# The second transform of a spectral and MLP mixer: radix 4 ahead of its products, or radix 2 ahead of them and radix 2 behind

## Chip, cores and metric

The kernel runs on one core of one Trainium2 chip. The time is in device microseconds for one execution. TensorE multiplies matrices, VectorE and ScalarE work element by element, SyncE (SP) issues the loads and stores. "Before" is the kernel as it stands, "after" the one with the change.

## What is computed

The input x has 2048 rows (the sequence) of 512 columns, all bf16. Two branches are mixed by a gate:

```python
g = sigmoid((x * gate_w).sum(-1, keepdims=True))
X = rfft2(x.astype(float32)) * (w_r + 1j * w_i)
a = irfft2(X, s=(2048, 512)).astype(bfloat16)
h = layernorm(x)
u = gelu(einsum("bsd,sf->bdf", h, w1) + b1)          # F = 1792
b = (einsum("bdf,fs->bds", u, w2) + b2).transpose(0, 2, 1)
out = g * a + (1 - g) * b
```

The rfft2 is a transform over the 2048 rows and one over the 512 columns. Both are done as products with tables of cosines and sines, with butterflies (additions and subtractions) around them that make the products shorter.

## The kernel before

Everything is bf16 in SBUF and fp32 in PSUM. x lies as four groups q by four remainders r by 512 columns, 128 rows in the partitions. A list of tasks is built in Python, each with an engine, an estimated duration, a priority and what it reads and writes (`Plan`, `add`). `order()` runs through these estimates and fixes the order in which each engine's instructions are written; the engines then run in that order and wait for each other through semaphores. So an edit of one task, or of its estimate, can move others.

The stages, with the names that matter here:

- **Statistics and h** (L478 to L513): mean and variance by VectorE, h mostly by ScalarE.
- **First transform** (over the rows): VectorE forms sums over q (L519 to L526, into a part of `gl`); TensorE multiplies for each r and each quarter dq of the columns (`fa`, L538 to L541), a quarter being 128 neighbouring columns; ScalarE evicts into X (L544).
- **Radix 4 over the quarters** (d4a, d4b: L551, L552, L557, L558): four additions or subtractions of 1024, 1024, 512 and 512 elements per partition for each r, in X itself and in `st`.
- **Radix 4 over r** (`radix4`, L577 to L590, once for each half lt of the frequencies, lt 1 first; L602 to L628 put the corner values right). Its results e = 0 to 3 stand in X in this order.
- **Second transform** (over the columns), `fb`: for each lt, e and c (real or imaginary part) four products, L646, L647 and twice L649, with 128, 128, 256 and 256 columns of the table `tb`; the two L649 accumulate. They write blocks of 64 columns into one bank of PSUM. ScalarE evicts each group into B and interleaves the four blocks (L653). The sixteen groups use the banks `fa` and `fb` in turn.
- **Spectral products**, all on VectorE for each lt: corner values to c0 (L770, L771), butterfly (L799, L800), preparation of W (L756 to L760, once), the multiplication by W (L807), combination (L812, L813), butterfly back (L819 to L821), then the inverse radix 4 over r (`radix4` again, L577 to L593, on B).
- **Inverse transforms**: products over the rows (L868 to L875), evictions (L881, L883), additions (L891 to L904), products over the columns (L942 to L946), evictions with the gate (L955), output additions ("es", L966 to L970).
- **MLP**: the products with w1 (L684: 14 tiles ft of the hidden width, 16 products of 512 columns each) and GELU (L700) run through the first half of the time. The products with w2 (L983: 14 for each of 16 row tiles) run through the second. Both are what the order puts between the transforms' products. `wa` and `wb` hold first w1 and then w2: SP loads w2's blocks i = 7 to 13 into `wb` when the products with the earlier contents are through.
- **Gate**: x times gate_w on VectorE (L709), sums on ScalarE (L714). The output of the MLP is scaled by ScalarE (L989), added (L995), and for the last tiles scaled and added by VectorE straight from PSUM (L1001), then stored.

Of the kernel before, what the change touches and what calls it, by code (L numbers as in the profile page):

```python
# [34 lines left out]
def make_tables():  # L35
# [49 lines left out]
                    u[:, P] = c[:, P] if lt == 0 else -n[:, P]  # L85
    ti[0, 2816:2945] = np.append(alt, 1.0)

    tb = np.zeros((P, 3, 4, 64))
    i = np.arange(64)
    for b in (0, 2):  # L90
        th = ang(p, b + 4 * i, D)
        tb[:, 0, b // 2] = np.cos(th)
        tb[:, 1, b // 2] = -np.sin(th)
    tb[:, 1, 0, 0] = alt
    tb[:, 2, 0:2] = tb[:, 0, 0:2]
    tc = np.zeros((P, 2, 3, 2, 64))
    for n, b in enumerate((1, 3)):
        th = ang(p, b + 4 * i, D)
        sg = 1.0 if b == 1 else -1.0
        tc[:, 0, 0, n] = np.cos(th)  # L100
        tc[:, 0, 1, n] = -np.sin(th)
        tc[:, 1, 0, n] = -sg * np.sin(th)
        tc[:, 1, 1, n] = -sg * np.cos(th)
    tc[:, :, 2] = tc[:, :, 0]
    cf = np.zeros((P, 4, 2))
    m = np.arange(8).reshape(4, 2)
    for r in range(4):
# [4 lines left out]
            cf[m[2, 0], r, 1], cf[m[3, 0], r, 1] = 1.0, (1.0, -1.0)[r % 2]  # L112
        if r != 0:
            cf[m[2, 1], r, 1], cf[m[3, 1], r, 1] = (0.0, -1.0, 1.0, 1.0)[r], (0.0, -1.0, -1.0, 1.0)[r]
    tb = np.concatenate([tb[:, :, 0:2].reshape(P, 384), tc.reshape(P, 768), cf.reshape(P, 8)], 1)

    tg = np.zeros((P, 642))
    sc = 2.0 / (D * S)
# [149 lines left out]
def kernel(  # L268
# [134 lines left out]
        dma(t["b1b"][0:NFT], B_b1.rearrange("(t f) -> t f", f=P))  # L403
        dma(t["b2b"][0:4], B_b2.rearrange("(q n) -> q n", q=4))
    add("SP", 1.0, ld_bias, writes=["bias"], prio=7.1, nbytes=16384, after=[a0])
    load("tb", [P, 1160], BF16, tabs["tb"], 296960, prio=9)

    def ld_wb(k, q):
        def emit():
# [46 lines left out]
        dma(t["ti"][:], tabs["ti"])  # L456
    load("tg", [P, 642], BF16, tabs["tg"], 164352, prio=29)


    HACT = set(range(NJ)) - {0, 8, 4}  # L460
    PQ0 = -0.5
    ASTAT = {12, 8}
    for r in range(4):
# [69 lines left out]
        for dq in range(4):  # L533
            def fa(r=r, dq=dq):
                pa = t["pa", r, dq] = ps([P, 2, 2, P], F32, "fa", 2)
                ta = t["ta"][:, r, :]
                w = lambda k: t["xf", r][:, k, dq * P:(dq + 1) * P]
                T.matmul(pa[:, 1], lhsT=w(2), rhs=ta[:, 256:512], start=True, stop=False)  # L538
                T.matmul(pa[:, 1], lhsT=w(3), rhs=ta[:, 384:640], start=False, stop=True)
                T.matmul(pa[:, 0, :, 0:64], lhsT=w(0), rhs=ta[:, 0:128], start=True, stop=True)  # L540
                T.matmul(pa[:, 0, :, 64:128], lhsT=w(1), rhs=ta[:, 128:256], start=True, stop=True)  # L541
            add("PE", mm(128, 128, 256, 256), fa, reads=[("xf", r % 2), ("ta", r)], writes=[("pa", r, dq)], prio=0, alloc=["fa"],
                free=["xf"] if dq == 3 else ())
            add("ACT", act(512), lambda r=r, dq=dq: A.copy(t["X"][:, :, r, :, dq, :], t["pa", r, dq][:]),  # L544
                reads=[("pa", r, dq)], writes=[("X", r, dq)], prio=0, free=["fa"])

        def d4a(r=r):
            xv = t["X"][:, :, r]
            s = t["st"][:, 1024:2048].rearrange("p (a c n) -> p a c n", a=2, c=2)
            two = lambda lo: xv[:, :, :, lo:lo + 2, :].rearrange("p a c j l -> p a c (j l)")  # L550
            V.tensor_add(s, two(0), two(2))  # L551
            V.tensor_sub(two(2), two(0), two(2))  # L552

        def d4b(r=r):
            xv = t["X"][:, :, r]
            s = t["st"][:, 1024:2048].rearrange("p (a c n) -> p a c n", a=2, c=2)
            V.tensor_add(xv[:, :, :, 0, :], s[:, :, :, 0:P], s[:, :, :, P:2 * P])  # L557
            V.tensor_sub(xv[:, :, :, 1, :], s[:, :, :, 0:P], s[:, :, :, P:2 * P])  # L558
        add("DVE", 2 * tt(1024), d4a, reads=[], writes=[("X", r, dq) for dq in range(4)] + ["sx"], prio=3.9)
        add("DVE", 2 * tt(512), d4b, reads=["sx"], writes=[("D", r)], prio=3.9)  # L560


    def radix4(view, pq, st, pqk, stk, reads, writes, prio, inverse):
        n = 512

        def parts(buf):
            v = buf().rearrange("p (m c n) -> p m c n", m=2, c=2)
            return v[:, 0], v[:, 1]

        def dst(lo, step):  # L570
            d = view().rearrange("p k c n -> p (k c) n")
            return d[:, lo:lo + step + 1:step]

        def e1():
            v = view()
            lo, hi = (v[:, 2 * i:2 * i + 2].rearrange("p m c n -> p (m c n)") for i in range(2))
            V.tensor_add(pq(), lo, hi)  # L577
            V.tensor_sub(st(), lo, hi)  # L578

        def e2():  # L580
            p, q = parts(pq)
            V.tensor_add(dst(0, 1), p, q)
            V.tensor_sub(dst(4, 1), p, q)

        def e3():
            s, u = parts(st)
            sr, ur = s[:, ::-1], u[:, ::-1]
            if not inverse:
                V.tensor_add(dst(2, 5), s, ur)
                V.tensor_sub(dst(3, 3), sr, u)  # L590
            else:
                V.tensor_add(dst(3, 3), sr, u)
                V.tensor_sub(dst(2, 5), s, ur)  # L593
        add("DVE", 2 * tt(4 * n), e1, reads=reads, writes=[pqk, stk], prio=prio)
        add("DVE", 2 * tt(2 * n), e2, reads=[pqk] + reads, writes=[writes[0]], prio=prio)
        add("DVE", 2 * tt(2 * n), e3, reads=[stk] + reads, writes=[writes[1]], prio=prio)

# [8 lines left out]
    def sp1():  # L606
# [3 lines left out]
        V.tensor_sub(sd[:, 1], sp[:, 0:2], sp[:, 2:4])  # L610
        V.tensor_add(fx[:, 0, 0], sd[:, 0, 0, 0], sd[:, 0, 1, 0])
        V.tensor_sub(fx[:, 0, 1], sd[:, 0, 0, 0], sd[:, 0, 1, 0])
        V.tensor_copy(fx[:, 1, 0], sd[:, 1, 0, 0])
        V.tensor_scalar_mul(fx[:, 1, 1], sd[:, 1, 1, 0], -1.0)
        V.tensor_scalar_mul(sd[:, 0, 0, 1], sd[:, 1, 1, 1], c)
        V.tensor_scalar_mul(sd[:, 1, 0, 1], sd[:, 0, 1, 1], -c)
        V.tensor_add(fx[:, 2, 0], sp[:, 0, 1], sd[:, 0, 0, 1])
        V.tensor_sub(fx[:, 3, 0], sp[:, 0, 1], sd[:, 0, 0, 1])
        V.tensor_sub(fx[:, 2, 1], sd[:, 1, 0, 1], sp[:, 2, 1])
        V.tensor_add(fx[:, 3, 1], sd[:, 1, 0, 1], sp[:, 2, 1])  # L620
    add("DVE", tiny(12), sp1, reads=["sp"], writes=["fx"], prio=0)

    for lt in (1, 0):
        pr = 3.0 if lt else 3.1
        radix4(lambda lt=lt: t["X"][:, lt].rearrange("p r c j l -> p r c (j l)"),
               lambda: t["xp"][:, 0:2048], lambda: t["st"][:, 0:2048], "xs", "st",
               dk + ([] if lt else ["sp"]), [("Z", lt, 0), ("Z", lt, 1)], pr, False)
    add("DVE", 0.15, lambda: V.tensor_copy(t["X"][:, 0, :, :, :, 0], t["fx"][:]), reads=["fx"],  # L628
        writes=[("Z", 0, 0), ("Z", 0, 1)], prio=3.1)

    def tbl(kind, c):
        tb = t["tb"]
        if kind < 2:
            return tb[:, 0:384].rearrange("p (c k i) -> p c k i", c=3, k=2)[:, c:c + 2, kind, :]
        v = tb[:, 384:1152].rearrange("p (g n) -> p g n", g=2)[:, kind - 2]
        return v[:, 128 * c:128 * c + 256]

    for lt in (0, 1):
        for e in (0, 2, 1, 3):
            for c in range(2):  # L640
                tag = ("fa", "fb")[c]

                def fb(lt=lt, e=e, c=c, tag=tag):
                    pb = t["pb", lt, e, c] = ps([P, 2, 4, 64], F32, tag, 2)
                    w = lambda k: t["X"][:, lt, e, c, k, :]
                    T.matmul(pb[:, :, 0, :], lhsT=w(0), rhs=tbl(0, c), start=True, stop=True)  # L646
                    T.matmul(pb[:, :, 2, :], lhsT=w(1), rhs=tbl(1, c), start=True, stop=True)  # L647
                    for k in (2, 3):
                        T.matmul(pb[:, :, 1::2, :], lhsT=w(k), rhs=tbl(k, c), start=(k == 2), stop=(k == 3))  # L649
                add("PE", mm(128, 128, 256, 256), fb, reads=[("Z", lt, e % 2), "tb"], writes=[("pb", lt, e, c)], prio=2, alloc=[tag])  # L650

                def fbev(lt=lt, e=e, c=c):
                    A.copy(t["B"][:, lt, e, 2 * c:2 * c + 2, :].rearrange("p s (i b) -> p s i b", b=4),  # L653
                           t["pb", lt, e, c][:].rearrange("p s b i -> p s i b"))
                add("ACT", act(512), fbev, reads=[("pb", lt, e, c)], writes=[("B", lt, e)], prio=1.8, free=[tag])


    def biasT():
# [105 lines left out]
    for lt in range(2):  # L764
# [8 lines left out]
        if lt == 0:  # L773
            def nyq():
# [6 lines left out]
                V.tensor_sub(nn[:, 0], na[:, 0, 1], na[:, 1, 0])  # L781
                V.tensor_add(nn[:, 1], na[:, 1, 1], na[:, 0, 0])
                V.tensor_mul(nn[:, :, 0], t["c0"][0:1, 0, 0, 1, :], wn[:, 0, 0:257:256])
            add("DVE", 3 * d1(512) + 0.1, nyq, reads=bk + [("W", 0), ("W", 1), ("c0", 0)] + pbk, writes=["nn"], prio=0.5)

        def c0b(lt=lt):
            c0, cm, ce, pm = t["c0"][:, lt], t["cm"], t["ce"][:, lt], t["wpm"]
# [46 lines left out]

    def linem():
        pl8 = t["pl8"] = ps([8, D], F32, "fa", 2)
        T.matmul(pl8[:], lhsT=t["tb"][:, 1152:1160], rhs=t["s9"][:], start=True, stop=True)
    add("PE", mm(512), linem, reads=["s9", "tb"], writes=["pl8"], prio=3, alloc=["fa"], after=[combt])
    add("ACT", act(512), lambda: A.copy(t["s8"][:], t["pl8"][:]), reads=["pl8"], writes=["s8"], prio=1.7, free=["fa"])

# [205 lines left out]
```

## Time and profile before

| | before |
|---|---|
| runs (us) | 132.31, 132.51, 132.73; median 132.51 |
| profiled execution | 132.39 us, of which the span of the trace is 130.5 |
| mean granted TensorE clock | 0.997 |
| ScalarE busy | 83.1 us |
| HBM read and written | 20.93 MB and 2.10 MB |

Times within the trace count from the start of the span. A busy time is the sum of the instructions' durations; two products overlap, so the distance from start to start ("pitch") is shorter than a duration. The rows of L646 and L649, for instance, have a mean duration of 219 and 272 ns. An idle time stands in brackets behind the instruction that ended it, with what it waited for. A line of the slices has 40 digits, each for 3.26 us, in tenths.

### The profile page before, as it was taken

The page shows a single profiled execution, that of the slowest core. Times are in us where ns is not written, and L with a number is a line of the kernel's source. Part 1 is how long each engine was busy: PE and PEld are TensorE (multiplying, and loading weights), DVE is VectorE, ACT ScalarE, POOL GpSimd, SP SyncE. Part 2 cuts the span into 40 slices and gives each one's busy share as a digit, 9 for nine tenths or more (in the row PEclk, how much of TensorE's full clock was granted, in tenths as well). Part 3 has the DMA queues.
Part 4 walks back from the last instruction along what each step waited for, and adds up shares of the span by engine and source line. Part 5 has one row for each costly group of instructions (what it writes and reads, how often), then busy time and mean ns, then how long its engine had stood idle before and what let it go on. Part 6 is the DMA issues. An engine that isn't in the chain of part 4 may idle for free.

```text
span 130.5 us, 2166 instructions
## 1 busy us (share of the span) xinstructions
PE 125.4 (96%) x780; PEld 70.7 (54%) x780; DVE 110.6 (85%) x248; ACT 83.1 (64%) x166; POOL 0.2 (0%) x4
## 2 busy tenths in 40 slices
PE   6998999999999999999999999999999999999991
PEld 2344565545544484854444555455687577655590
DVE  2689999999999997059999999999959929999961
ACT  4468989599999999996111044322499489962200
POOL 0000000000000000000000000000000000000000
PEclk9999999999999999999999999999999999999998
DMA  4999999943669536799999800000000000312331
GB/s 83 389 372 386 398 394 379 374 91 89 135 184 298 107 85 131 259 288 406 414 421 421 334 6 0 3 5 3 0 0 0 0 5 0 161 69 97 161 121 40
DMA packets 17478, 23.18 MB, mean 178 GB/s; under 512 B 1574, under 2 KB 14908, under 8 KB 17468
## 3 DMA queue, kind: packets, MB, share of 16 engines
q1 hardware_dynamic: 17180, 22.59, 50.6%
q10 hardware_dynamic: 288, 0.46, 1.3%
q8 instruction: 6, 0.10, 0.3%
q14 instruction: 4, 0.03, 0.1%
HBM read 20.93 MB, written 2.10 MB: 176 GB/s over the span
## 4 chain that ended last, share of the span: by engine, by line
PE 58%; DVE 28%; DMA 8%; issue 2%; ACT 2%; SPq 0%; DVEq 0%
PE acc L684 18%; PE acc L983 17%; DMA wa<-in_B_w_dram 5%; PE fb L684 5%; DVE xp L807 3%; DVE st L807 3%; DMA x<-in_A_x_dram 2%; PE fa L684 2%; PE fa L538 2%; DVE xp L812 2%; DVE st L578 2%; DVE B L819 2%; DVE xp L813 2%; PE fb L868 1%; PE fa L868 1%
## 5 line engine op out<-in xcount | busy, mean ns | idle before, releaser
L983 PE MATMUL acc<-gl,wb 128*128 128x512 bf16 (+1 forms) x112 | 27.4, 373 | 0.0
L983 PE MATMUL acc<-gl,wa 128*128 128x512 bf16 (+1 forms) x112 | 27.2, 372 | 0.0
L684 PE MATMUL acc<-h,wb 128*128 128x512 bf16 x112 | 25.9, 379 | 0.0
L989 ACT ACTIVATE x<-acc,ombb,omg 128x512 bf16<-128x512 f32 x14 | 10.8, 785 | 22.7 <-PE acc L983 22.7
L983 PEld LDWEIGHTS <-wb 128*128 128x128 bf16 x126 | 13.4, 114 | 10.3 <-DMA wb<-in_B_w_dram 1.2
L983 PEld LDWEIGHTS <-wa 128*128 128x128 bf16 x126 | 13.5, 114 | 9.4
L684 PE MATMUL acc<-h,wa 128*128 128x512 bf16 x64 | 17.8, 387 | 0.6 <-DVE h L505 0.6
L684 PEld LDWEIGHTS <-wb 128*128 128x128 bf16 x112 | 10.9, 98 | 11.7
L684 PEld LDWEIGHTS <-wa 128*128 128x128 bf16 x112 | 10.4, 99 | 10.8 <-issue 2.1
L700 ACT ACTIVATE gl<-acc,b1f 128x512 bf16<-128x512 f32 x11 | 7.6, 693 | 6.8 <-PE acc L684 6.8
L478 DVE BATCH_NORM_STATS2 stats<-x 128x6 f32<-128x512 bf16 x14 | 9.4, 674 | 2.2 <-DMA x<-in_A_x_dram 2.2
L544 ACT CAST X<-fa 128x512 bf16<-128x512 f32 x16 | 9.3, 582 | 2.7 <-PE fa L541 2.5
L511 ACT ACTIVATE h<-x,nmr,rstd 128x512 bf16<-128x512 bf16 x13 | 9.8, 806 | 0.4 <-DVE nmr L502 0.2
L714 ACT ACTIVATE x<-x 128x512 bf16<-128x512 bf16 x16 | 10.1, 655 | 0.0
L684 PE MATMUL fb<-h,wa 128*128 128x512 bf16 x32 | 9.4, 379 | 0.0
L955 ACT ACTIVATE B<-fb,g 128x512 bf16<-128x512 f32 x8 | 5.9, 735 | 0.0
L955 ACT ACTIVATE B<-fa,g 128x512 bf16<-128x512 f32 x8 | 5.8, 727 | 0.0
L359 PE MATMUL fa<-xp 128*128 128x512 bf16 x10 | 4.4, 632 | 1.2 <-DVE xp L320 1.2
L684 PE MATMUL fa<-h,wa 128*128 128x512 bf16 x16 | 5.6, 379 | 0.0
L653 ACT CAST B<-fb 128x512 bf16<-128x512 f32 x8 | 5.0, 628 | 0.0
L653 ACT CAST B<-fa 128x512 bf16<-128x512 f32 x8 | 4.9, 616 | 0.0
L709 DVE TENSOR_TENSOR x<-x,gw 128x2048 bf16<-128x2048 bf16 x4 | 4.8, 1216 | 0.0
(177 smaller groups left out, 230.0 us busy)
## 6 DMA issues: line engine op xcount, KB each, us to landing
wb<-in_B_w_dram SPq DMA_DIRECT2D x11, 512.0 KB
wa<-in_B_w_dram SPq DMA_DIRECT2D x7, 512.0 KB
wa<-in_B_w_dram SPq DMA_DIRECT2D x3, 896.0 KB
x<-in_A_x_dram SPq DMA_DIRECT2D x3, 512.0 KB
wb<-in_B_w_dram SPq DMA_DIRECT2D x4, 384.0 KB
out_dram<-x SPq DMA_DIRECT2D x3, 512.0 KB
rot<-dft_ti SPq DMA_DIRECT2D x1, 736.5 KB
rot<-dft_ta SPq DMA_DIRECT2D x4, 160.0 KB
```

The source lines that it names most:

```text
L478: V.bn_stats(out=t["stats"][:, j, :], in_=t["x"][:, j // 4, j % 4, :])
L511: add("ACT", 0.71, lambda j=j: A.activation(t["h"][:, j // 4, j % 4, :], t["x"][:, j // 4, j % 4, :], ActF.Identity, bias=t["nmr"][:, j:j ...
L544: add("ACT", act(512), lambda r=r, dq=dq: A.copy(t["X"][:, :, r, :, dq, :], t["pa", r, dq][:]), reads=[("pa", r, dq)], writes=[("X", r, dq ...
L653: A.copy(t["B"][:, lt, e, 2 * c:2 * c + 2, :].rearrange("p s (i b) -> p s i b", b=4), t["pb", lt, e, c][:].rearrange("p s b i -> p s i b"))
L684: T.matmul(t["u", ft][:], lhsT=w[:, j // 4, j % 4, c * P:(c + 1) * P], rhs=t["h"][:, j // 4, j % 4, :], start=(j == jorder[0]), stop=(j == ...
L700: gelus.append(add("ACT", act(512, 1) , lambda ft=ft: A.activation(t["gl"][:, ft, :], t["u", ft][:], ActF.Gelu_apprx_tanh, bias=t["b1f"][: ...
L709: add("DVE", tt(2048), lambda r=r: V.tensor_mul(t["x"][:, :, r, :], t["x"][:, :, r, :], t["gw"][:, None, :].to_broadcast([P, 4, D])), read ...
L714: A.activation(t["x"][:, q, r, :], t["x"][:, q, r, :], ActF.Copy, accum_out=t["glog"][:, 4 * q + r:4 * q + r + 1])
L807: V.tensor_mul(o, xs, w)
L955: A.activation(t["eo", j // 2][:, j % 2], t["i3", j][:], ActF.Copy, scale=t["g"][:, j:j + 1])
L983: T.matmul(t["y", j, n][:, cs], lhsT=w[:, o, 512 * q + r:512 * q + 512:4], rhs=t["gl"][:, ft, cs], start=(ft == 0), stop=(ft == NFT - 1))
L989: A.activation(tbuf(j).rearrange("p h d -> p (h d)"), t["y", j, 0][:], ActF.Identity, bias=t["ombb2"][:, j:j + 1], scale=t["omg"][:, j:j + 1])
```

## The change

In the second transform the index of the 512 columns is split as 256h + 2p + t (h and t are 0 or 1, p the partition). The first transform takes for its weights every second column (t) of one half (h) instead of 128 neighbouring columns, and is evicted into `xp` instead of X. VectorE then does a radix 2 over h alone (`d2`), from `xp` into X. The products of `fb` are four with 128 columns each, none accumulating, and each writes every second fp32 column of its 256. The evictions go back into X, and each waits for the products of both c. A radix 2 over t (`tb2`) then forms B from X: one addition of 1024 elements, two subtractions of 508 that write in reversed order, and, once per lt, six operations on the corner values. Radix 4 over r stores its results as 0, 2, 1, 3, and does lt 0 first. `tb` has 776 columns instead of 1160.

```diff
-                w = lambda k: t["xf", r][:, k, dq * P:(dq + 1) * P]
+                w = lambda k: t["xf", r][:, k, L * (dq // 2) + dq % 2:L * (dq // 2 + 1):2]
...
-            add("ACT", act(512), lambda r=r, dq=dq: A.copy(t["X"][:, :, r, :, dq, :], t["pa", r, dq][:]),
+            add("ACT", act(512), lambda r=r, dq=dq: A.copy(xe(r)[:, :, :, dq, :], t["pa", r, dq][:]),
...
-        add("DVE", 2 * tt(1024), d4a, reads=[], writes=[("X", r, dq) for dq in range(4)] + ["sx"], prio=3.9)
-        add("DVE", 2 * tt(512), d4b, reads=["sx"], writes=[("D", r)], prio=3.9)
+        def d2(r=r):
+            e, xv = xe(r), t["X"][:, :, r]
+            for i in range(2):
+                V.tensor_add(xv[:, i, :, 0:2], e[:, i, :, 0:2], e[:, i, :, 2:4])
+                V.tensor_sub(xv[:, i, :, 2:4], e[:, i, :, 0:2], e[:, i, :, 2:4])
+        add("DVE", 4 * tt(512), d2, reads=[("X", r, dq) for dq in range(4)], writes=[("D", r)], prio=3.9)
...
-    for lt in (1, 0):
-        pr = 3.0 if lt else 3.1
+    for lt in (0, 1):
+        pr = 3.0 + 0.1 * lt
...
-                    pb = t["pb", lt, e, c] = ps([P, 2, 4, 64], F32, tag, 2)
-                    w = lambda k: t["X"][:, lt, e, c, k, :]
-                    T.matmul(pb[:, :, 0, :], lhsT=w(0), rhs=tbl(0, c), start=True, stop=True)
-                    T.matmul(pb[:, :, 2, :], lhsT=w(1), rhs=tbl(1, c), start=True, stop=True)
-                    for k in (2, 3):
-                        T.matmul(pb[:, :, 1::2, :], lhsT=w(k), rhs=tbl(k, c), start=(k == 2), stop=(k == 3))
+                    pb = t["pb", lt, e, c] = ps([P, 2, 2, P], F32, tag, 2)
+                    for k in range(4):
+                        T.matmul(pb[:, k % 2, :, k // 2::2], lhsT=t["X"][:, lt, EX[e], c, k, :], rhs=tbl(k, c), start=True, stop=True)
...
-                    A.copy(t["B"][:, lt, e, 2 * c:2 * c + 2, :].rearrange("p s (i b) -> p s i b", b=4),
-                           t["pb", lt, e, c][:].rearrange("p s b i -> p s i b"))
-                add("ACT", act(512), fbev, reads=[("pb", lt, e, c)], writes=[("B", lt, e)], prio=1.8, free=[tag])
+                    A.copy(t["X"][:, lt, EX[e]].rearrange("p c j l -> p (c j l)").rearrange("p (h c g) -> p h c g", h=2, c=2)[:, :, c],
+                           t["pb", lt, e, c][:].rearrange("p h s l -> p h (s l)"))
+                add("ACT", act(512), fbev, reads=[("pb", lt, e, i) for i in range(2)], writes=[("R", lt, e, c)], prio=1.8, free=[tag])
+
+            if e >= 2:
+                def tb2(lt=lt, e0=e - 2):
+                    b = t["B"][:, lt]
+                    v = t["X"][:, lt].rearrange("p e c j l -> p e (c j l)").rearrange("p e (h w l) -> p e h w l", h=2, w=4)
+                    bh, vh = b[:, e0::2], v[:, 2 * e0:2 * e0 + 2]
+                    V.tensor_add(bh[:, :, :, 0:P], vh[:, :, 0], vh[:, :, 1])
+                    V.tensor_sub(bh[:, :, 0:4:3, L - 1:P:-1], vh[:, :, 0, 0:4:3, 1:P], vh[:, :, 1, 0:4:3, 1:P])
+                    V.tensor_sub(bh[:, :, 1:3, L - 1:P:-1], vh[:, :, 1, 1:3, 1:P], vh[:, :, 0, 1:3, 1:P])
...
+                es_ = (e - 2, e) if e == 2 else (0, 1, 2, 3)
+                add("DVE", tt(1024) + 2 * tt(508) + tiny(6) * (e > 2), tb2, reads=[("R", lt, i, c) for i in (e - 2, e) for c in range(2)],
+                    writes=[("B", lt, i) for i in es_], prio=2.5)
```

More of the change, by code (lines that the diff above doesn't have):

```diff
@@ L86, in make_tables @@
     ti[0, 2816:2945] = np.append(alt, 1.0)
[L88 to L104, printed above, removed]
+    tb = np.zeros((P, 2, 2, 3, 64))
+    for par in range(2):
+        for h in range(2):
+            th = ang(2 * p + h, par + 2 * np.arange(64), D)
+            tb[:, par, h, 0] = np.cos(th)
+            tb[:, par, h, 1] = -np.sin(th)
+            if par == 0:
+                tb[:, 0, h, 1, 0] = (alt, -alt)[h]
+            tb[:, par, h, 2] = tb[:, par, h, 0]
     cf = np.zeros((P, 4, 2))
@@ L114, in make_tables @@
             cf[m[2, 1], r, 1], cf[m[3, 1], r, 1] = (0.0, -1.0, 1.0, 1.0)[r], (0.0, -1.0, -1.0, 1.0)[r]
-    tb = np.concatenate([tb[:, :, 0:2].reshape(P, 384), tc.reshape(P, 768), cf.reshape(P, 8)], 1)
+    tb = np.concatenate([tb.reshape(P, 768), cf.reshape(P, 8)], 1)
     tg = np.zeros((P, 642))
@@ L405 @@
     add("SP", 1.0, ld_bias, writes=["bias"], prio=7.1, nbytes=16384, after=[a0])
-    load("tb", [P, 1160], BF16, tabs["tb"], 296960, prio=9)
+    load("tb", [P, 776], BF16, tabs["tb"], 198656, prio=9)
     def ld_wb(k, q):
@@ L457, with xe @@
     load("tg", [P, 642], BF16, tabs["tg"], 164352, prio=29)
+    def xe(r):
+        return t["xp"][:, 2048 * r:2048 * r + 2048].rearrange("p (a c j l) -> p a c j l", a=2, c=2, j=4)
     HACT = set(range(NJ)) - {0, 8, 4}
@@ L543 @@
                 free=["xf"] if dq == 3 else ())
-            add("ACT", act(512), lambda r=r, dq=dq: A.copy(t["X"][:, :, r, :, dq, :], t["pa", r, dq][:]),
+            add("ACT", act(512), lambda r=r, dq=dq: A.copy(xe(r)[:, :, :, dq, :], t["pa", r, dq][:]),
                 reads=[("pa", r, dq)], writes=[("X", r, dq)], prio=0, free=["fa"])
[L547 to L558, printed above, removed]
-        add("DVE", 2 * tt(1024), d4a, reads=[], writes=[("X", r, dq) for dq in range(4)] + ["sx"], prio=3.9)
-        add("DVE", 2 * tt(512), d4b, reads=["sx"], writes=[("D", r)], prio=3.9)
+        def d2(r=r):
[4 more added lines that the diff above has]
+        add("DVE", 4 * tt(512), d2, reads=[("X", r, dq) for dq in range(4)], writes=[("D", r)], prio=3.9)
     def radix4(view, pq, st, pqk, stk, reads, writes, prio, inverse):
@@ L582, in e2 @@
             V.tensor_add(dst(0, 1), p, q)
-            V.tensor_sub(dst(4, 1), p, q)
+            V.tensor_sub(dst(4, 1) if inverse else dst(2, 1), p, q)
         def e3():
@@ L588, in e3 @@
             if not inverse:
-                V.tensor_add(dst(2, 5), s, ur)
-                V.tensor_sub(dst(3, 3), sr, u)
+                V.tensor_add(dst(4, 3), s, ur)
+                V.tensor_sub(dst(5, 1), sr, u)
             else:
@@ L612, in sp1 @@
         V.tensor_sub(fx[:, 0, 1], sd[:, 0, 0, 0], sd[:, 0, 1, 0])
-        V.tensor_copy(fx[:, 1, 0], sd[:, 1, 0, 0])
-        V.tensor_scalar_mul(fx[:, 1, 1], sd[:, 1, 1, 0], -1.0)
+        V.tensor_copy(fx[:, 2, 0], sd[:, 1, 0, 0])
+        V.tensor_scalar_mul(fx[:, 2, 1], sd[:, 1, 1, 0], -1.0)
         V.tensor_scalar_mul(sd[:, 0, 0, 1], sd[:, 1, 1, 1], c)
         V.tensor_scalar_mul(sd[:, 1, 0, 1], sd[:, 0, 1, 1], -c)
-        V.tensor_add(fx[:, 2, 0], sp[:, 0, 1], sd[:, 0, 0, 1])
+        V.tensor_add(fx[:, 1, 0], sp[:, 0, 1], sd[:, 0, 0, 1])
         V.tensor_sub(fx[:, 3, 0], sp[:, 0, 1], sd[:, 0, 0, 1])
-        V.tensor_sub(fx[:, 2, 1], sd[:, 1, 0, 1], sp[:, 2, 1])
+        V.tensor_sub(fx[:, 1, 1], sd[:, 1, 0, 1], sp[:, 2, 1])
         V.tensor_add(fx[:, 3, 1], sd[:, 1, 0, 1], sp[:, 2, 1])
     add("DVE", tiny(12), sp1, reads=["sp"], writes=["fx"], prio=0)
-    for lt in (1, 0):
-        pr = 3.0 if lt else 3.1
+    for lt in (0, 1):
+        pr = 3.0 + 0.1 * lt
         radix4(lambda lt=lt: t["X"][:, lt].rearrange("p r c j l -> p r c (j l)"),
@@ L627 @@
                dk + ([] if lt else ["sp"]), [("Z", lt, 0), ("Z", lt, 1)], pr, False)
-    add("DVE", 0.15, lambda: V.tensor_copy(t["X"][:, 0, :, :, :, 0], t["fx"][:]), reads=["fx"],
-        writes=[("Z", 0, 0), ("Z", 0, 1)], prio=3.1)
+        if lt == 0:
+            add("DVE", 0.15, lambda: V.tensor_copy(t["X"][:, 0, :, :, :, 0], t["fx"][:]), reads=["fx"],
+                writes=[("Z", 0, 0), ("Z", 0, 1)], prio=3.0)
+    EX = (0, 2, 1, 3)
     def tbl(kind, c):
[L632 to L636, printed above, removed]
+        return t["tb"][:, 192 * kind + 64 * c:192 * kind + 64 * c + P].rearrange("p (s i) -> p s i", s=2)
     for lt in (0, 1):
@@ L650 @@
-                add("PE", mm(128, 128, 256, 256), fb, reads=[("Z", lt, e % 2), "tb"], writes=[("pb", lt, e, c)], prio=2, alloc=[tag])
-                def fbev(lt=lt, e=e, c=c):
-                    A.copy(t["B"][:, lt, e, 2 * c:2 * c + 2, :].rearrange("p s (i b) -> p s i b", b=4),
-                           t["pb", lt, e, c][:].rearrange("p s b i -> p s i b"))
-                add("ACT", act(512), fbev, reads=[("pb", lt, e, c)], writes=[("B", lt, e)], prio=1.8, free=[tag])
+                    pb = t["pb", lt, e, c] = ps([P, 2, 2, P], F32, tag, 2)
@@ new lines, in fb @@
+                    for k in range(4):
+                        T.matmul(pb[:, k % 2, :, k // 2::2], lhsT=t["X"][:, lt, EX[e], c, k, :], rhs=tbl(k, c), start=True, stop=True)
+                add("PE", mm(128, 128, 128, 128), fb, reads=[("Z", lt, e % 2), "tb"], writes=[("pb", lt, e, c)], prio=2, alloc=[tag])
+            for c in range(2):
+                tag = ("fa", "fb")[c]
+                def fbev(lt=lt, e=e, c=c):
+                    A.copy(t["X"][:, lt, EX[e]].rearrange("p c j l -> p (c j l)").rearrange("p (h c g) -> p h c g", h=2, c=2)[:, :, c],
+                           t["pb", lt, e, c][:].rearrange("p h s l -> p h (s l)"))
+                add("ACT", act(512), fbev, reads=[("pb", lt, e, i) for i in range(2)], writes=[("R", lt, e, c)], prio=1.8, free=[tag])
@@ new lines @@
+            if e >= 2:
[6 more added lines that the diff above has]
+                    V.tensor_sub(bh[:, :, 1:3, L - 1:P:-1], vh[:, :, 1, 1:3, 1:P], vh[:, :, 0, 1:3, 1:P])
+                    if e0:
+                        for i in range(2):
+                            bh, vh = b[:, i::2], v[:, 2 * i:2 * i + 2]
+                            V.tensor_sub(bh[:, :, 1:3, 0], vh[:, :, 0, 0:4:3, 0], vh[:, :, 1, 0:4:3, 0])
+                            V.tensor_copy(bh[:, :, 0:4:3, P], vh[:, :, 0, 1:3, 0])
+                            V.tensor_copy(bh[:, :, 1:3, P], vh[:, :, 1, 1:3, 0])
+                es_ = (e - 2, e) if e == 2 else (0, 1, 2, 3)
+                add("DVE", tt(1024) + 2 * tt(508) + tiny(6) * (e > 2), tb2, reads=[("R", lt, i, c) for i in (e - 2, e) for c in range(2)],
+                    writes=[("B", lt, i) for i in es_], prio=2.5)
@@ L783, in nyq @@
                 V.tensor_mul(nn[:, :, 0], t["c0"][0:1, 0, 0, 1, :], wn[:, 0, 0:257:256])
-            add("DVE", 3 * d1(512) + 0.1, nyq, reads=bk + [("W", 0), ("W", 1), ("c0", 0)] + pbk, writes=["nn"], prio=0.5)
+            add("DVE", 3 * d1(512) + 0.1, nyq, reads=[("B", i, e) for i in range(2) for e in range(4)] + [("W", 0), ("W", 1), ("c0", 0)] + pbk, writes=["nn"], prio=0.5)
         def c0b(lt=lt):
@@ L836, in linem @@
         pl8 = t["pl8"] = ps([8, D], F32, "fa", 2)
-        T.matmul(pl8[:], lhsT=t["tb"][:, 1152:1160], rhs=t["s9"][:], start=True, stop=True)
+        T.matmul(pl8[:], lhsT=t["tb"][:, 768:776], rhs=t["s9"][:], start=True, stop=True)
     add("PE", mm(512), linem, reads=["s9", "tb"], writes=["pl8"], prio=3, alloc=["fa"], after=[combt])
```

## The prediction

> **What bounds the kernel now.** I read the busy shares and slices of the page first, then the timeline engine by engine, then the waits.
>
> ```profile
> PE 125.4 (96%) x780; PEld 70.7 (54%) x780; DVE 110.6 (85%) x248; ACT 83.1 (64%) x166; POOL 0.2 (0%) x4
> PE   6998999999999999999999999999999999999991
> DVE  2689999999999997059999999999959929999961
> ```
>
> TensorE has no empty slice from 10 us to the end. Its busy time counts overlaps, so I count starts. In the timeline of TensorE:
>
> ```profile
> 45.42 0.22 PE L646 MATMUL fa<-tb,X 128*128 128x128 bf16 x1
> 45.48 0.22 PE L647 MATMUL fa<-tb,X 128*128 128x128 bf16 x1
> 45.53 0.38 PE L649 MATMUL fa<-tb,X 128*128 128x256 bf16 x2
> 45.75 0.22 PE L646 MATMUL fb<-tb,X 128*128 128x128 bf16 x1
> ...
> 116.75 1.67 PE L983 MATMUL acc<-gl,wb 128*128 128x512 bf16 x7
> 118.26 1.67 PE L983 MATMUL acc<-gl,wa 128*128 128x512 bf16 x7
> ```
>
> Starts lie 0.055 us apart behind 128 columns, 0.109 behind 256 (45.53 to 45.75 holds two) and 0.2157 behind 512 (1.51 for seven). Summing these pitches over the order of the program, from the L684 at 10.23 to the end of the last product, gives 115.5 us; the trace has 117.2 (to 127.4). So 1.65 us of that stretch is waiting (0.83 before 31.6, 0.07 to 68.0, 0.40 to 92.8, 0.34 at 94.8, by where the starts fall behind the sum) and the rest is columns: **the number of columns sets the end.** A column removed counts if no other chain moves in.
>
> Two others run close behind. VectorE, from the timeline and the waits:
>
> ```profile
> 51.40 0.25 DVE L628 CAST X<-fx 128x32 bf16<-128x32 f32 x1
> 56.51 0.17 DVE L770 CAST c<-B 128x8 f32<-128x8 bf16 x1 [4.86 <-ACT B L653]
> ...
> 94.78 0.23 PE L872 MATMUL fb<-rot,B 128*128 128x128 bf16 x1 [0.17 <-DVE B L593]
> ...
> 124.54 0.74 DVE L1001 SCALAR_TENSOR_TENSOR x<-acc,omg,x 128x512 bf16<-128x512 f32 x1
> 126.03 0.48 DVE L1001 SCALAR_TENSOR_TENSOR x<-acc,omg,x 128x256 bf16<-128x256 f32 x1 [0.75 <-PE acc L983]
> 127.59 0.35 DVE L1001 SCALAR_TENSOR_TENSOR x<-fb,omg,x 128x128 bf16<-128x128 f32 x1 [0.43 <-PE fb L983]
> ```
>
> It is idle 4.86 us before the spectral products, then works without a hole to 94.7; the inverse transform waits for it at 94.78, and at the end it waits for TensorE. The other is the load of w2:
>
> ```profile
> PEld L983 <- DMA wb<-in_B_w_dram: 1.2, 4, 0.4
> ```
>
> From 60 to 73 us the transfers run at 408 to 424 GB/s, saturated, and TensorE takes each block as it lands.
>
> **The change, part by part.**
>
> *Products of the second transform.* Sixteen groups of 128+128+256+256 = 768 columns become 4 x 128 = 512. Each group's start-to-start is 0.33 now (45.42 to 45.75) and will be 4 x 0.055 = 0.22. Gain 16 x 0.109 = **1.74 us of TensorE**. With the regrouped rest, the sum of pitches over the new order is 1.70 less. Weight loads stay 64. The first transform now reads its stationary operand at every second column; L868 and L872 do so already and their loads take 98 ns like the plain ones, so nothing.
>
> The unknown is that each product now writes every second fp32 column. No row has this. The nearest, L646 and L649, write blocks of 64 with gaps at the full 0.055 and 0.109, so a gap between blocks is free; lower end: no cost. Upper end: a column as long as two, which is the 256-column row, 0.109 instead of 0.055, 64 x 0.054 = +3.5 us. I take zero, by the nearer row, and keep the other end as a rival. [...]
>
> *VectorE ahead of the products.* Out: per r L551, L552 (0.60 pitch each) and L557, L558 (0.34), with a 0.12 wait, 2.0 us, four times 8.0. In: four adds of 512 elements, 4 x 0.34 = 1.36, four times 5.4. So 2.6 less. But the last r still waits for its evictions: the new order issues the gate products (L709, 4 x 1.14) before it, and its L541 comes some 0.9 us later on TensorE, so its eviction ends near 37.4. VectorE will idle about 1.5 us there and begin the last radix 2 at 37.4. Adding 1.36, the corner values 0.1 + 1.1, and one radix 4 of 4.7 (2 x 1.14 + 4 x 0.60) plus 0.2 for the copy gives 45.05 for the first half. TensorE's order asks for it as its 231st product, as now, at 45.4: no stall.
>
> *VectorE behind the products.* In: four times 0.60 + 0.34 + 0.34 = 1.28 (L820's kind and L968's, which reads from an odd column and writes reversed) and twice six tiny operations at 0.08, with two waits, 0.55. Together **6.2 us**. They fall into the idle 4.86 us and into the 2.6 saved. By the new order: second radix 4 starts at 45.05; the first lt 0 part stands in it, ahead of its last two operations, and so ahead of the products of lt 1, e 1 and 3: it would hold them if its evictions were late, but they end at 48.0 and it is due at 48.5. Radix 4, both lt 0 parts and the lt 0 corner are done at 52.85. ScalarE evicts the sixteen groups nearly in one run (0.476 each, as at L653, one GELU of 0.6 between) from 46.05 to 54.3, against 56.9 now, as the second half no longer stands behind gate sums. The lt 1 parts then end at 54.1 and, after the last eviction, 56.3; then L799 and L800 (2.27), 58.6; the second corner copy, 58.8. Now W's preparation (L756) starts at 59.34. So the spectral chain is **0.5 us earlier**. If that cover were gone and all 6.2 us came on top, it would start at over 65 and the inverse transform would wait.
>
> *Evictions.* Their number and size stay; they wait for both halves of a pair (0.1 at the first). Off the path. The table tb is 98 KB smaller, at about 390 GB/s 0.25 us of an early transfer no engine waits for.
>
> *What is late next.* TensorE comes to L983 1.71 us earlier, at 66.3 instead of 68.02. Its eighth weight block is asked at 67.8. Blocks land every 1.24 us by the load waits (69.74, 70.97, 72.22), so the eighth is there at about 68.3 to 68.5 (SP queues the wb blocks when ft 10 is through, now 57.92, then 57.4, but the saturated transfer gives little of it back). I expect about 0.5 us of stall there, against 0.40 now; the later blocks are asked 6 or 7 matmuls (1.3 to 1.5 us) apart and are in time. The order puts 118 products of L983 instead of 112 ahead of the inverse transform, so TensorE reaches lt 1 of it at 94.15, and VectorE is ready at 94.78 - 0.5 = 94.3: 0.15 lost instead of 0.34. Then ScalarE's sixteen evictions, the last transform and the output adds follow at the same spacing, about 0.5 us earlier; the last L1001 on VectorE could start at about 125.4 and TensorE ends its last product near 125.6.
>
> *Sum.* -1.70 columns, +0.1 at w2, -0.2 at the inverse transform: -1.8 at best. VectorE's tail has only 0.2 us left and my reading of the landings is good to about 0.3, so I take **-1.6**. The profiled execution took 132.39 with a span of 130.5; 132.39 - 1.6 = **130.8**. The median shown is 132.51, 0.1 above it. This case alone runs from 130.4 to 131.3.
>
> **The rivals.**
>
> 1. *Every second column costs double on the write.* One mechanism: 64 products at 0.109 are 7.0 us instead of 5.24 now. TensorE passes the second transform 1.74 us later than now instead of 1.74 earlier. Both waits, 0.74, disappear (the w2 blocks are there, VectorE is ready first), so the end moves by +1.74 + 0.04 for the other pitches - 0.74 = +1.05, to **133.5**. It decides from the point where the extra per product passes (1.70 + 0.1) / 64, some 28 ns, half its present pitch. Against it: L649's blocks. For it: no row writes single columns. [...]
>
> 2. *The gain is swallowed by the other chains.* If the eighth block lands at 68.9 and the radix-2 additions run 0.6 us longer than booked, TensorE loses another 0.4 at w2 and 0.6 at the inverse transform: 131.8. VectorE's tail says the same from its side: with its chain as late as now, its last L1001 follows the others without a wait at 125.95 instead of 127.59, a gain of 1.6; 1 us later than now leaves 0.6. For it: VectorE is full from 57 to 125. Against it: the 4.86 idle, and that the order releases the last eviction 2.6 us sooner.
>
> 3. *The change doesn't shorten the products.* Excluded by its order of instructions: all 64 write 128 columns.
>
> **How the numbers follow.** Forecast (130.4 to 131.3) 0.55; rival 2 (131.3 to 132.8) 0.13, of which 0.06 within 0.3% of now; rival 1 (132.9 to 134.2) 0.32. About 0.3%, 0.4 us, is what a measurement of this kernel can tell from no change. So faster 0.62, same 0.06, slower 0.32. The range goes from 130.4 up to 133.8, which takes in most of rival 1.
>
> **What would show it.** The product line with pitch 0.055 and busy 218 ns: the columns came out; a pitch of 0.109: rival 1. VectorE's hole at 51.7 should shrink to pieces under 0.5 us and a new one of about 1.5 us stand near 36. The spectral multiply (63.81 now) should start near 63.3. The first w2 wait should stand at the eighth block, about 0.5 us. The prediction fails if the first spectral multiply is later than now, or if the transfer wait is over 1 us.

## The result and the profile after

The change makes the kernel slower: 134.21 us, median of 4 runs (134.09 to 134.29), against 132.49 (4 runs, 132.31 to 132.73); the ratio is 1.0131, interval 1.0117 to 1.0145. Forecast were 130.8; what came is the first rival, somewhat dearer than priced. The profiled execution after took 134.28 us, its span is 132.4 (before: 132.39 and 130.5), the granted clock 0.999.

The page's busy times after:

```profile
PE 126.9 (96%) x780; PEld 72.8 (55%) x780; DVE 114.1 (86%) x272; ACT 84.2 (64%) x166; POOL 0.2 (0%) x4
```

TensorE is as full as before, with as many instructions, and 1.5 us busier, although the change takes 4096 columns of products out. The timeline of TensorE after (start, duration, engine, line, form, count) says where they went:

```profile
45.86 0.60 PE L632 MATMUL fa<-tb,X 128*128 128x128 bf16 x4
46.25 0.64 PE L632 MATMUL fb<-tb,X 128*128 128x128 bf16 x4
46.69 0.64 PE L632 MATMUL fa<-tb,X 128*128 128x128 bf16 x4
47.12 0.64 PE L632 MATMUL fb<-tb,X 128*128 128x128 bf16 x4
...
70.00 1.67 PE L987 MATMUL acc<-gl,wa 128*128 128x512 bf16 x7
...
128.80 0.55 PE L987 MATMUL fb<-gl,wb 128*128 128x128 bf16 x7
```

A group of four products of 128 columns goes from 46.25 to 46.69: 0.109 us each, what 256 columns took before, not 0.055. The last seven products begin at 128.80; before they began at 127.00:

```profile
127.00 0.55 PE L983 MATMUL fb<-gl,wb 128*128 128x128 bf16 x7
```

VectorE after:

```profile
37.82 0.43 DVE L545 TENSOR_TENSOR X<-xp 128x512 bf16<-128x512 bf16 x1 [0.95 <-ACT xp L539]
...
55.30 0.69 DVE L648 TENSOR_TENSOR B<-X 128x1024 bf16<-128x1024 bf16 x1 [1.97 <-ACT X L639]
...
57.81 0.69 DVE L648 TENSOR_TENSOR B<-X 128x1024 bf16<-128x1024 bf16 x1 [1.00 <-ACT X L639]
...
66.91 2.27 DVE L811 TENSOR_TENSOR xp<-xp,W 128x4096 bf16<-128x4096 bf16 x1
```

The hole near 36 is there (0.95, and 0.55 before 30.23). The hole before the spectral products has not shrunk to pieces under 0.5 us: the additions of radix 2 wait 1.97 and 1.00 us for evictions, which themselves wait for slow products (L639 for L632, 1.5 us in four waits). So the spectral multiply (L811, before L807) starts 3.1 us later than before, not 0.5 earlier. Before, it stood here:

```profile
63.81 2.27 DVE L807 TENSOR_TENSOR xp<-xp,W 128x4096 bf16<-128x4096 bf16 x1
```

### The profile page after: what moved, and what is told of

The parts are those of the page before. It is cut to its first block, busy times and chain, and to the rows that moved or that the text cites. A ratio compares the mean times of both kernels' runs of the same rounds, so it can differ in the third digit from the quotient of the medians.

```text
span 132.4 us, 2192 instructions
## 1 busy us (share of the span) xinstructions
PE 126.9 (96%) x780; PEld 72.8 (55%) x780; DVE 114.1 (86%) x272; ACT 84.2 (64%) x166; POOL 0.2 (0%) x4
## 4 chain that ended last, share of the span: by engine, by line
PE 90%; DVE 3%; DMA 3%; ACT 2%; issue 0%
PE acc L987 35%; PE acc L688 28%; PE fb L688 5%; PE fb L632 3%; PE fa L632 3%; DMA x<-in_A_x_dram 3%; PE fa L688 2%; PE fa L533 2%; PE fa L872 1%; PE fb L872 1%; PE fa L534 1%; PE fa L536 1%; PE fa L535 1%; ACT h L478 1%; PE fb L987 1%; PE fa L987 1%
## 5 line engine op out<-in xcount | busy, mean ns | idle before, releaser
L987 PE MATMUL acc<-gl,wb 128*128 128x512 bf16 (+1 forms) x112 | 28.3, 372 | 0.0
L688 PE MATMUL acc<-h,wb 128*128 128x512 bf16 x112 | 26.5, 382 | 0.0
L688 PE MATMUL acc<-h,wa 128*128 128x512 bf16 x64 | 17.2, 379 | 1.0 <-DVE h L500 0.9
L539 ACT CAST xp<-fa 128x512 bf16<-128x512 f32 x16 | 9.3, 581 | 2.9 <-PE fa L536 2.7
L632 PEld LDWEIGHTS <-X 128*128 128x128 bf16 x64 | 6.9, 130 | 1.7
L639 ACT CAST X<-fa 128x512 bf16<-128x512 f32 x8 | 4.7, 588 | 1.8 <-PE fb L632 1.5
L648 DVE TENSOR_TENSOR B<-X 128x1024 bf16<-128x1024 bf16 x4 | 2.8, 690 | 3.0 <-ACT X L639 3.0
```

Of the source, the lines that this page charges most:

```text
L539: add("ACT", act(512), lambda r=r, dq=dq: A.copy(xe(r)[:, :, :, dq, :], t["pa", r, dq][:]), reads=[("pa", r, dq)], writes=[("X", r, dq)], ...
L632: T.matmul(pb[:, k % 2, :, k // 2::2], lhsT=t["X"][:, lt, EX[e], c, k, :], rhs=tbl(k, c), start=True, stop=True)
L639: A.copy(t["X"][:, lt, EX[e]].rearrange("p c j l -> p (c j l)").rearrange("p (h c g) -> p h c g", h=2, c=2)[:, :, c], t["pb", lt, e, c][:] ...
L688: T.matmul(t["u", ft][:], lhsT=w[:, j // 4, j % 4, c * P:(c + 1) * P], rhs=t["h"][:, j // 4, j % 4, :], start=(j == jorder[0]), stop=(j == ...
L987: T.matmul(t["y", j, n][:, cs], lhsT=w[:, o, 512 * q + r:512 * q + 512:4], rhs=t["gl"][:, ft, cs], start=(ft == 0), stop=(ft == NFT - 1))
```

## The experiments

Two theories stood against each other. A: a product that writes every second fp32 column takes twice the time, TensorE's columns set the end, and that is all. Its closer form, a price by lines of two neighbouring fp32 columns, no run had shown at that point: the kernel after has the doubling at step 2 (0.109) and nothing finer; e2 and e3 put it to the test. B: the time is lost in the regrouped work around the products (evictions that wait for pairs, 6.2 us more of VectorE behind them), and the slow pitch is a symptom.

For all of them, one measure in the traces is steadier than the time: the stretch from TensorE's first product of the second transform to the start of its last seven products. What lies ahead of it varies with the landing of the first load, for which VectorE waited 2.2 us before, 2.4 after and 2.5 in "corrected plan". The medians come from several chips: the kernel before took 132.94 us beside "contiguous" and "corrected plan", 132.44 beside "no corners", and 132.50 beside the other runs that follow "after". The stretch is taken from one profiled execution of each.

| kernel | first product | first with w2 | start of the last seven | stretch | median (us) |
|---|---|---|---|---|---|
| before | 45.42 | 68.02 | 127.00 | 81.58 | 132.49 |
| after | 45.86 | 70.00 | 128.80 | 82.94 | 134.21 |
| after, again | 45.63 | 69.78 | 128.58 | 82.95 | 134.25 |
| contiguous | 45.82 | 66.62 | 125.42 | 79.60 | 131.22 |
| contiguous, again | 45.89 | 66.67 | 125.48 | 79.59 | 130.83 |
| half strided | 45.64 | 68.08 | 126.88 | 81.24 | 132.37 |
| corrected plan | 45.91 | 70.16 | 128.84 | 82.93 | 134.32 |
| more VectorE | 46.02 | 66.90 | 128.17 | 82.15 | 133.41 |
| no corners | 45.64 | 66.43 | 125.83 | 80.19 | 130.99 |

### The contiguous write (e1_contig, e1b_contig)

```diff
-                        T.matmul(pb[:, k % 2, :, k // 2::2], lhsT=t["X"][:, lt, EX[e], c, k, :], rhs=tbl(k, c), start=True, stop=True)
+                        T.matmul(pb[:, k % 2, k // 2, :], lhsT=t["X"][:, lt, EX[e], c, k, :], rhs=t["tb"][:, 192 * k + 64 * c:192 * k + 64 * c + P], start=True, stop=True)
...
-                    A.copy(t["X"][:, lt, EX[e]].rearrange("p c j l -> p (c j l)").rearrange("p (h c g) -> p h c g", h=2, c=2)[:, :, c],
-                           t["pb", lt, e, c][:].rearrange("p h s l -> p h (s l)"))
+                    A.copy(t["X"][:, lt, EX[e]].rearrange("p c j l -> p (c j l)").rearrange("p (h c n b) -> p h c n b", h=2, c=2, b=2)[:, :, c],
+                           t["pb", lt, e, c][:].rearrange("p h b n -> p h n b"))
```

> The changed kernel with one thing undone: each product writes 128 neighbouring accumulator columns, and ScalarE's eviction brings the even and odd columns together, as the eviction before did with its four blocks. The order of instructions is the changed kernel's on every engine. Theory A (the write of every second column costs double): L632 at a pitch of 0.055 us instead of 0.109, 64 x 0.054 = 3.5 us of TensorE columns come out; the first spectral multiply goes from 66.91 to about 63.3, the wait for w2 comes back at the eighth block (about 0.5 us), and the end falls to 130.8, at most 131.3. Theory B (the time is lost in the regrouped VectorE and ScalarE work, evictions that wait for pairs and 6.2 us more behind the products, and the pitch is only what TensorE shows while it is held): the pitch may change, the time stays within 133.8 to 134.5. Between the two, 131.5 to 133.5, both act.

131.22 us beside 132.94 on its chip, ratio 0.9842 (0.9786 to 0.9898). TensorE's timeline and VectorE's in this kernel:

```profile
45.82 0.39 PE L632 MATMUL fa<-tb,X 128*128 128x128 bf16 x4
46.05 0.39 PE L632 MATMUL fb<-tb,X 128*128 128x128 bf16 x4
...
125.42 0.55 PE L987 MATMUL fb<-gl,wb 128*128 128x128 bf16 x7
```

```profile
54.94 0.69 DVE L648 TENSOR_TENSOR B<-X 128x1024 bf16<-128x1024 bf16 x1 [0.28 <-ACT X L639]
...
63.53 2.27 DVE L811 TENSOR_TENSOR xp<-xp,W 128x4096 bf16<-128x4096 bf16 x1
```

0.055 again, 3.34 us out of the stretch (52 ns for each of 64 products), the hole down to 0.28, the multiply at 63.53. Theory B falls: every instruction stands where it stood after, only the columns' places differ. That ScalarE now interleaves costs nothing here: its evictions start 0.47 to 0.48 us apart, as before and after. The expected wait for w2 did not come (below).

Once more, on one chip with the changed kernel and two that follow (e5, e6):

> The contiguous write once more, beside the changed kernel. If the price of the writes is all that separates the two, it lies 64 x 0.0537 = 3.4 us, give or take 0.2 of waits, under the changed kernel, and 0.986 to 0.989 of the kernel before (its TensorE ended at 125.81 instead of 127.39, 1.6 us earlier, with 0.4 us lost at the first loads that the kernel before can lose too).

> The changed kernel itself once more, on the same chip as the next three, so that they can be set against it. 1.012 to 1.015 of the kernel before, as the first time.

130.83 us, ratio 0.9866 (0.982 to 0.9912); after: 134.25, ratio 1.0114 (1.0069 to 1.0159). The distance is 3.42 us. This version beats both kernels.

### The stride alone, in the kernel before (e2_before_step4)

```diff
-                    pb = t["pb", lt, e, c] = ps([P, 2, 4, 64], F32, tag, 2)
+                    pb = t["pb", lt, e, c] = ps([P, 2, 64, 4], F32, tag, 2)
...
-                    T.matmul(pb[:, :, 0, :], lhsT=w(0), rhs=tbl(0, c), start=True, stop=True)
-                    T.matmul(pb[:, :, 2, :], lhsT=w(1), rhs=tbl(1, c), start=True, stop=True)
+                    T.matmul(pb[:, :, :, 0], lhsT=w(0), rhs=tbl(0, c), start=True, stop=True)
+                    T.matmul(pb[:, :, :, 2], lhsT=w(1), rhs=tbl(1, c), start=True, stop=True)
...
-                        T.matmul(pb[:, :, 1::2, :], lhsT=w(k), rhs=tbl(k, c), start=(k == 2), stop=(k == 3))
+                        T.matmul(pb[:, :, :, 1::2].rearrange("p s i n -> p s n i"), lhsT=w(k), rhs=tbl(k, c), start=(k == 2), stop=(k == 3))
```

> The kernel before with one thing put in: its products write every fourth accumulator column (the four parts interleaved in the bank) and ScalarE reads the bank straight through. Theory A, as one fp32 value for each line of two: 128 columns at 0.109 and 256 at 0.216, so 16 groups of 0.655 instead of 0.327, 5.2 us more of TensorE; less the 0.74 us of waits that such a delay covers, the end goes from 132.4 to 136.5 to 137.2. If the price grows with the step (four columns of reach, not two), the pitches are 0.218 and 0.436 and the time is over 145. Theory B (the pattern of the write is no cost by itself): 132.4 as before.

137.11 us, ratio 1.0272 (1.0191 to 1.0354): theory A without the rest of the change. In its timeline of TensorE

```profile
46.58 0.31 PE L646 MATMUL fb<-tb,X 128*128 128x128 bf16 x1
46.69 0.31 PE L647 MATMUL fb<-tb,X 128*128 128x128 bf16 x1
46.80 0.64 PE L649 MATMUL fb<-tb,X 128*128 128x256 bf16 x2
47.23 0.31 PE L646 MATMUL fa<-tb,X 128*128 128x128 bf16 x1
```

128 columns take 0.11 and two times 256 take 0.43; four columns of reach cost what two do.

### The price by itself (e3_micro)

Twenty patterns, 32 products each, for instance

```python
for n in range(32): T.matmul(B[n % 8][:, 0:256:2], lhsT=w(n), rhs=m, start=True, stop=True)   # L46
for n in range(32): T.matmul(v(n, "p (i k) -> p i k", k=8)[:, 0:32, 1:5], lhsT=w(n), rhs=m, start=True, stop=True)   # L60
```

> Leaves the reference's computation out: 32 products of 128 x 128 by 128 columns for each of twenty patterns, each pattern on its own line, nothing else beside them. Contiguous columns: 0.055 us. Theory A, by lines of two fp32 values (one value at a time for each line costs a whole line): steps of 2, 3 and 4 all 0.109, pairs that fill a line 0.055, pairs that begin at an odd column 0.109, blocks of four from an odd column 0.082 (three lines for four values), contiguous from an odd column 0.056, 64 columns at step 2 0.055 and 256 at step 2 0.216. A second reading, that any gap costs: pairs and fours with gaps also 0.109. A third, that only the length of the reach counts: step 4 0.218. Reversed columns and two blocks written in turn are open: 0.055 if the write joins whatever falls into one line, 0.109 if only neighbours in ascending order are joined. Stride on the moving operand (steps 2 and 4) and on the stationary one (2 and 3): no change, 0.055, by the first transform's strided loads at the plain 98 ns.

Its timeline of TensorE; a line is one pattern, the distance to the next start over 32 is the pitch:

```profile
14.11 1.95 PE L42 MATMUL b<-x 128*128 128x128 bf16 x32
15.90 1.98 PE L44 MATMUL b<-x 128*128 128x128 bf16 x32
17.71 3.66 PE L46 MATMUL b<-x 128*128 128x128 bf16 x32
21.16 3.70 PE L48 MATMUL b<-x 128*128 128x128 bf16 x32
24.66 3.70 PE L50 MATMUL b<-x 128*128 128x128 bf16 x32
28.15 3.70 PE L52 MATMUL b<-x 128*128 128x128 bf16 x32
31.64 1.99 PE L54 MATMUL b<-x 128*128 128x128 bf16 x32
33.47 3.66 PE L56 MATMUL b<-x 128*128 128x128 bf16 x32
36.92 1.99 PE L58 MATMUL b<-x 128*128 128x128 bf16 x32
38.75 2.80 PE L60 MATMUL b<-x 128*128 128x128 bf16 x32
41.37 1.97 PE L62 MATMUL b<-x 128*128 128x128 bf16 x32
43.18 3.66 PE L64 MATMUL b<-x 128*128 128x128 bf16 x32
46.63 1.14 PE L66 MATMUL b<-x 128*128 128x64 bf16 x32
...
59.75 2.05 PE L74 MATMUL b<-x 128*128 128x128 bf16 x32
61.64 3.87 PE L76 MATMUL b<-x 128*128 128x128 bf16 x32
65.34 1.97 PE L78 MATMUL b<-x 128*128 128x128 bf16 x32
```

| written columns (128 values) | line | pitch (ns) |
|---|---|---|
| contiguous; from an odd column | L42; L44 | 56; 57 |
| every second; the odd ones | L46; L48 | 108; 109 |
| every third; every fourth | L50; L52 | 109; 109 |
| pairs with gaps, from an even column; from an odd one | L54; L56 | 57; 108 |
| fours with gaps, from an even column; from an odd one | L58; L60 | 57; 82 |
| contiguous, in descending order | L62 | 57 |
| two blocks of 64, one column of each in turn | L64 | 108 |

This is one execution, with a mean granted clock of 0.949; from 14 us on its contiguous pitch, 56 ns, is that of the kernels (55). 64 values at step 2 take 55 ns (contiguous 30) and 256 take 215 (contiguous 110). The pitches fit a count of lines of two fp32 columns, aligned at even ones: 128 single columns touch 128 lines, 128 contiguous ones 64, fours from an odd column 96 (82 ns, one and a half times 55). A gap as such is free (L54 and L58: 57 ns). Only neighbours in time are joined: L64 fills every line in the end, and pays double (108). On the operands' side, the stationary one at step 2 or 3 costs nothing here (L78 at step 2: 56; L80 at step 3, which nothing follows, is as busy as L42, 1.95 us), the moving one costs 59 at step 2 (L74) and 116 at step 4 (L76), which I had expected at 55.

### Half the products (e5_half)

The contiguous kernel, with the `k // 2::2` write back for lt 0 only.

> The contiguous kernel with the stride put back in one half: the 32 products of lt 0 write every second column, the 32 of lt 1 neighbouring ones. Theory A (each strided column costs one more, and TensorE's columns set the end): 32 x 0.0537 = 1.72 us over the contiguous kernel, halfway to the changed one, within 0.3; that is the break-even of the forecast's first rival (27 ns for each product on the average, 28 named), so the time comes out within 0.4 us of the kernel before. Theory B (the loss needs a chain that slips as a whole, the evictions and VectorE behind the products): not halfway; within 0.5 us of the contiguous kernel, as ScalarE's evictions of 0.47 us each are slower than half the products anyway.

132.37 us, ratio 0.9982 (0.996 to 1.0005): 1.54 over the contiguous kernel on the same chip, 1.88 under the changed one, and not to be told from before. The stretch, 81.24, lies at 79.59 + 1.65, half of 3.36 being 1.68. With 0, 32 and 64 strided products the stretch is 79.59, 81.24 and 82.95: the cost is linear in the products, and 27 ns for each on the average is the break-even.

### The planner's estimate (e4_plan)

```diff
-                add("PE", mm(128, 128, 128, 128), fb, reads=[("Z", lt, e % 2), "tb"], writes=[("pb", lt, e, c)], prio=2, alloc=[tag])
+                add("PE", mm(256, 256, 256, 256), fb, reads=[("Z", lt, e % 2), "tb"], writes=[("pb", lt, e, c)], prio=2, alloc=[tag])
```

> The changed kernel, its writes at every second column kept, but the planner counts each product at 256 columns, what the trace shows, instead of 128, and so writes another order for TensorE. The columns stay the same. If the gap between the priced 133.5 and the measured 134.2 comes from an order made for faster products, the end falls by some 0.3 to 0.7, to 133.5 to 133.9. If it comes from elsewhere (transfers before 10 us), 134.0 to 134.4.

134.32 us, ratio 1.009 (1.0047 to 1.0132): no gain in the time, within the upper of the two ranges. The ratio is lower than after's because the kernel before took 132.94 beside it. Yet the order moved VectorE much. Its timeline there:

```profile
63.39 2.29 DVE L811 TENSOR_TENSOR xp<-xp,W 128x4096 bf16<-128x4096 bf16 x1
```

The multiply starts 3.5 us earlier than after, and the stretch is 82.93 instead of 82.94. The new order also brings the inverse transform forward (its first product at 92.61 instead of 95.91), so this run moves more than VectorE. It shows that with the same columns an order in which VectorE is 3.5 us ahead ends no sooner: in the changed kernel VectorE's delay cost nothing that another order gave back.

### More and less on VectorE (e6_dve_more, e7_no_corner)

The contiguous kernel, with

```diff
                     V.tensor_add(bh[:, :, :, 0:P], vh[:, :, 0], vh[:, :, 1])
+                    V.tensor_add(bh[:, :, :, 0:P], vh[:, :, 0], vh[:, :, 1])
```

> The contiguous kernel with its longest new VectorE operation (L648, 0.60 us) issued twice in each of its four places, the second time with the same values: 2.4 us more VectorE work behind the products, TensorE's columns unchanged. By the forecast's second rival, VectorE's tail has 0.2 to 0.3 us left and the inverse transform already waits 0.3 for it: the first spectral multiply moves from 63.53 to 65.6 to 65.9, and the end by 1.5 to 2.2 us, to nearly the time before. If the columns alone set the end, because products of the second weight stand ready to fill such waits: less than 0.6 us.

133.41 us, ratio 1.0056 (1.0032 to 1.008): 2.58 over the contiguous kernel, more than either reading said. The work put in was also more than the 2.4 us expected: the first L648 starts at 49.16 and the line behind it at 49.88, so one more costs 0.72 us, not 0.60, and four cost 2.9. Of these 0.25 fell into VectorE's last wait for evictions (in "contiguous, again"), which is gone. The multiply starts at 66.28, 2.7 later, and TensorE stands still at the inverse transform, which the contiguous kernel passes with 0.33 us lost:

```profile
94.29 0.22 PE L877 MATMUL fa<-rot,B 128*128 128x129 bf16 x1 [1.33 <-DMA B<-s]
...
97.25 0.23 PE L877 MATMUL fb<-rot,B 128*128 128x128 bf16 x1 [0.97 <-DVE B L580]
```

The first of these waits is for a small transfer into B, which SP issues at 92.22, when VectorE (L580) releases it. So both waits go back to VectorE: here its chain carries the end.

And the other way, the six corner operations of each lt left out (`if e0:` made `if False:`):

> The contiguous kernel with VectorE's twelve small corner operations behind the products left out (so 4 of the 256 values of each row are wrong), 12 x 0.075 = 0.9 us less VectorE work at the same columns; one small fill at the start, where VectorE waits for its first load. The counterpart of the run with 2.4 us more. If both chains end together (TensorE waits 0.32 us at the inverse transform, all of it for VectorE), the spectral multiply moves 0.9 us earlier, to about 62.6, the 0.32 us go, and no more, since then the columns alone bind: 0.2 to 0.4 us under the contiguous kernel. If VectorE's chain carries the end by itself there, 0.9 us under it. If the waits at the inverse transform come from the evictions beside it and not from the spectral chain, no change.

130.99 us, ratio 0.9881 (0.9854 to 0.9908), on another chip than the contiguous runs (0.9842 and 0.9866): no change that can be told from them, and none of the three readings is shown. The multiply came only 0.25 us earlier than in "contiguous, again" (63.33 instead of 63.58), as much as the first product did, since VectorE then waited 0.60 for evictions and 0.34 for a gate sum. And the profiled execution, the slowest of the six (131.53; the others 130.61 to 131.40), lost time at w2:

```profile
68.63 0.41 PE L988 MATMUL acc<-gl,wb 128*128 128x512 bf16 x1 [0.53 <-DMA wb<-in_B_w_dram]
```

Here SP began to queue w2's `wb` blocks at 57.40, in both contiguous runs at 56.45 and 56.50. Why it was later is open (SP's `wa` blocks were late already, from 52.05 on instead of 51.11 and 51.55), and so is what less VectorE work would bring by itself: the quicker executions have no trace.

## Why the prediction was wrong

- **Products: the step that failed.** "I take zero, by the nearer row" for the write of every second fp32 column. The true price is the other end of that step's own bounds: 0.109 instead of 0.055. With 52 ns for 64 products, 3.35 us in the stretch, the columns came to +1.65 instead of -1.70. L646 and L649 were near in size and far in kind: their gaps lie between blocks that fill whole lines, so they could say nothing of lines half used.
- **What no row showed.** Before the result no row wrote single columns; that the nearer row held for them was the author's estimate. e3 shows the price by lines of two fp32 columns: pairs and fours from an even column run at 57 ns (L54, L58), pairs from an odd one at 108 (L56), two blocks written in turn at 108 (L64). By that the forecast would have been the first rival's.
- **VectorE ahead of the products: held, but for 0.4 us.** First half of X forecast for 45.05 (the terms listed for it add up to 44.86), ready at about 45.5 without a stall of TensorE; the hole of 1.5 us came as 0.95 and 0.55. TensorE began its products 0.4 us later than before, which I had not seen: 0.2 from the landing of the first load, which other executions of the order before had too (first product at 45.98 in e2), and 0.19 from a stop ahead of the product at 33.84 (33.6 to 34.0 in the other profiles of the new order), which the kernel before does not have there; its cause was not tried.
- **VectorE behind the products: right once the price is taken out.** 63.3 was forecast, the contiguous kernel has 63.53; after, 66.91.
- **What is late next: right in sum, wrong in parts.** In the contiguous kernel the 0.5 us at w2's eighth block did not come, as the blocks were queued at 56.45, not 57.4; with 57.40 in e7's profiled execution it came, 0.53. The inverse transform kept its 0.33 instead of 0.15. The parts cancelled: 1.98 saved in the stretch, 0.4 lost before it, profiled 131.05 and medians 131.22 and 130.83, with 130.8 forecast for this case.
- **First rival: the right mechanism, 0.7 too cheap.** I let both waits, 0.74 us, vanish. Of these 0.19 belong to a small product at 83.19 (L837) that waits after too (86.07), and 0.32 to the inverse transform, where VectorE slipped along with TensorE (after: 0.18 and 0.14). Only the w2 wait, 0.2, went. So 1.65 - 0.2 is about the 1.36 found in the stretch; 0.44 more were lost before it.
- **Second rival: did not act, but its mechanism is real.** With contiguous writes, 2.9 us more on VectorE cost 2.58 (e6). With the strided ones, e4's order had VectorE 3.5 us ahead and gained nothing.

## What to carry to other kernels

Where a product's result is interleaved, write contiguous columns (or aligned pairs, 57 ns in e3) and interleave in the eviction; here that turned +1.7 us into -1.7. A row bounds a new access pattern only if it shares what the pattern changes; when no row does, none of them is the nearer one, and both ends stay open: here the pitch was 0.109, not 0.055. When an engine's columns set the end, ask which second chain is level with it: here VectorE was (e6), and in one execution the w2 load (e7).

## What the runs showed of the hardware

- In e3 a product of 128 columns pays by the lines of two fp32 columns that it writes, in the order in which it writes them: 108 ns for single columns (L46), 82 for fours from an odd column (L60), 57 for contiguous ones in descending order (L62).
- A moving bf16 operand at step 4 takes 116 ns for 128 columns (L76 of e3), at step 2 it takes 59 (L74); a stationary operand at step 2 takes 56 (L78), like the plain one (L42).
